# Tile 7 of a window attention joins the tiles that take small scores and a turned exchange

## The chip, the cores and the metric

The kernel runs on one core of a Trainium2 chip. The core has five engines with a queue of instructions each: TensorE (PE: matmuls, its weight loads apart as PEld), VectorE (DVE), ScalarE (ACT), GpSimd (POOL), and SyncE (SP), which here issues all DMAs. The metric is the device time of one execution in microseconds (us). Three runs of the kernel before gave 554.05, 554.26 and 555.79 us; the median is 554.26.

## The reference

q, k and v have 8 batches, 8 heads, 576 tokens and 64 columns a head. Attention looks back at most 127 tokens, with a bias that falls linearly with distance; then comes a feed-forward part with a convolution of three tokens and a gate.

```python
scores = scale * np.matmul(q, k.transpose(0, 1, 3, 2))
mask = (rel >= 0) & (rel < 128)
scores = np.where(mask, scores - slopes * abs(rel), -1e9)
attn = softmax(scores); x = np.matmul(attn, v)      # heads side by side: 512 columns
h = np.maximum(x @ w_in, 0.0)                       # 512 -> 1024
conv = cw[0] * h[s-1] + cw[1] * h[s] + cw[2] * h[s+1]
out = (h * sigmoid(conv)) @ w_out                   # 1024 -> 512
```

## The kernel before, in words

The 8 x 576 tokens are 36 tiles of 128 tokens, numbered 0 to 35. A tile's attention is done in two halves of four heads, u = 0 and 1. Two tiles form a chunk of 256 tokens for the feed-forward part, and a chunk is done in four steps s, each of two blocks of 128 hidden columns. In the names of tiles, sc is scores, e the exponentials, av the product with v, p the up product, z the gate, gh and gl the high and low part of the gated values, o the output sums. The feed-forward products run as three fp32r products (high by high, high by low, low by high).

There are two ways to do a tile's attention.

- The whole way (tiles 0 to 7 before): scores are 128x128 matmuls over the tile's own keys and, in a second set, the tile before (`scores`, L398). VectorE merges the two by masks (L442). The exponentials are normalised, TensorE transposes them (`attnT`, L507), they are copied out of PSUM (`attn_out`), POOL selects what belongs to which tile (`select`), and TensorE multiplies with v over 128 keys (`av`, L631).
- The turned way (tiles 8 to 35 before): scores are matmuls of 32 queries over 160 keys (`scores_window`, L413), so that each query block sees the 160 keys that its window can touch. VectorE turns the exponentials in blocks of 32 (`turn_e`, L534), they are written to DRAM (`write_e`, L544: 1 MB) and read back in another arrangement by four DMAs (`swap_e`, L558), POOL selects (`select_e`, L568 and L572), and TensorE multiplies with v in quarters of the array (`av_quarters`, L591). The two halves of the sum are added on VectorE (`x_sum`, L605).

A third piece belongs to the turned tiles: q and k come as 32-row blocks and VectorE turns them (`turn`, from tile TURN on), where earlier tiles are transposed by TensorE (`qkT`).

The order of the work is written out by hand. OPENING covers tiles 0 to 10 and the weights' preparation, PERIOD is a loop over pairs of tiles from tile 8 on, TAIL the rest. Each word is a step and its arguments: S7.0 are the scores of tile 7, half 0; MP, MB its masks and bias; X exponentials; N normalisation; TE, WE, SE, CE the four steps of the exchange; AV the product with v; XA, XS, XH, XL the steps to the feed-forward input; UH up, HH relu, Z, CA and CB convolution, TH tanh, GT gate, GH and GL the high and low part, D down, OB output; F, CL, RS, LW, V, H and W weights; I a few filler matmuls; LG four loads of q and k. Each engine executes its own instructions in the order of these words, and the table OTHER says which steps run on a second engine instead of the usual one (`pick`). All DMAs stand in SP's queue, in order.

```python
def write_e(t):
    if t < FIRST:
        return
    ...
    nc.sync.dma_start(out=scrs[t][:P].rearrange("p n b f -> p n (b f)"), in_=eb)
```

FIRST (L142) is the first turned tile, and it set TURN (L289) and the loop's start too.

Of the kernel before, what the change touches and what calls it, by code (L numbers as in the profile page):

```python
# [22 lines left out]
def tile_alibi_window_attention_conv_glu(  # L23
# [855 lines left out]
    MB0.1.1 QU1.0 QU1.1 I2 QV1.0 I2 I2 LW0 MB0.1.0 S1.0 MP1.0.1 CL4 MP1.0.0 QV1.1 S1.1 MP1.1.0 MB1.1.0 MB1.0.1 QU2.1  # L879
    X0.0.0 X0.0.1 X0.1.1 X0.1.0 NR0 QV2.1 X1.1.0 N0.0 I1 I1 N0.1 X1.0.1 LW4 QU2.0 QV2.0 S2.1 MB1.0.0 CL0 S2.0  # L880
    MP1.1.1 X1.0.0 MB1.1.1 T0.1 RS4 X1.1.1 F1 CL1 LW1 MP2.1.1 MP2.0.0 MP2.0.1 NR1 T0.0 RL0.0 RL0.1 N1.1 N1.0 F2
    SEL0.0 V4 QU3.1 MB2.1.1 I1 I1 LV2 MB2.0.0 QV3.1 MP2.1.0 MB2.1.0 MB2.0.1 RS0 QU3.0 QV3.0 T1.1 P4 S3.1 SEL0.1
    MP3.1.0 MP3.1.1 RL1.1 MB3.1.0 SEL1.1 V0 S3.0 T1.0 RL1.0 LD4 QU4.0 X2.0.1 MB3.1.1 W4 I2 X2.1.1 CL2 MP3.0.1 X2.1.0
    QU4.1 LV0 X2.0.0 NR2 N2.1 N2.0 F3 AV0 XH0 QV4.1 QV4.0 MB3.0.1 H0 T2.0 RL2.0 LW3 X3.1.1 S4.0 MP3.0.0 MB3.0.0 T2.1
    LD5 S4.1 SEL1.0 CL3 SEL2.0 MP4.0.1 MB4.0.1 RL2.1 RS1 V1 RS3 RS2 LW2 MP4.0.0 SEL2.1 QU5.1 LV1 AV1 QV5.1 AV2 F6
    CL6 S5.1 XH1 QU5.0 MP4.1.0 MB4.1.0 X3.0.0 V3 X3.0.1 F8 MP4.1.1 MB4.1.1 MB4.0.0 CL8 X3.1.0 V2 F5 CL5 XH2 XL2 H1
    QV5.0 RS8 W1 LG4 UH1.0 NR3 N3.0 N3.1 MP5.1.1 UH1.1 X4.0.1 MP5.1.0 T3.1 HH1.0 X4.1.0 MB5.1.1 UH0.0 F7 CL7 LW5 W0
    MB5.1.0 F15 HH0.0 LW8 X4.1.1 X4.0.0 NR4 RL3.1 RS6 LD6 QU6.1 LW6 V6 LW7 RS7 V7 T3.0 QV6.1 V8 N4.0 LG4 LV4 RS5 V5
    HH1.1 RL3.0 SEL3.0 UH0.1 S5.0 MP5.0.0 HH0.1 LV3 F10 CL10 Z0.1 QU6.0 MP5.0.1 H7 F9 Z0.0 T4.0 RL4.0 H3 CA0.1 CB0.1
    LG4 UH3.0 HH3.0 N4.1 UH2.0 SEL4.0 CA0.0 T4.1 CB0.0 MB5.0.1 LD7 CL9 SEL3.1 X5.1.1 QV6.0 S6.0 MB5.0.0 HH2.0 TH0  # L890
    RL4.1 RS10 SEL4.1 X5.1.0 GT0 MP6.0.0 S6.1 MB6.0.0 Z1.0 MP6.0.1 AV3 H2 W3 X5.0.0 LW10 LG4 MP6.1.1 Z1.1 MB6.0.1
    LW9 AV4 H8 QU7.1 CA1.0 CB1.0 F12 LG4 X5.0.1 MP6.1.0 MB6.1.0 CA1.1 W2 CB1.1 NR5 N5.1 LV5 UH3.1 XH4 XL4 RS9 V9
    MB6.1.1 GL0 XH3 F11 TH1 LG4 LG4 X6.0.0 UH2.1 CL15 HH2.1 Z2.1 XL3 XF4 GT1 F13 LG4 QV7.1 Z2.0 F14 X6.1.1 H6 QU7.0
    QV7.0 CL11 RS11 LW11 V10 T5.1 CA2.0 CB2.0 RL5.1 W7 LG4 W8 HH3.1 UH4.1 UH4.0 CA2.1 CB2.1 TH2 CL12 F16 S7.1 RS12
    MP7.1.1 S7.0 X6.0.1 HH4 D0 GT2 GL1 Z3.1 N5.0 T5.0 MP7.0.1 W6 MB7.0.1 UH5.0 SEL5.1 UH5.1 H5 W5 UH7.0 CA3.1 KC7
    N6.0 LW15 UH7.1 Z3.0 CL16 CA3.0 CB3.0 CL13 LW12 CB3.1 MP7.0.0 MB7.0.0 TH3 GT3 LW16 Z4.1 GL3 CL14 LG4 MP7.1.0 V12
    LG4 HH5 MB7.1.0 X7.0.0 X6.1.0 V11 N6.1 LV8 MB7.1.1 LG4 H10 LW13 LV6 W10 RS16 BW1 UH6.1 CA4.1 CB4.1 Z4.0 X7.1.0
    CA4.0 CB4.0 T6.0 TQ8 LG4 X7.0.1 RL5.0 LG4 UH6.0 TH4 GT4 LG4 LG4 GL2 LG4 SEL5.0 RL6.0 SEL6.0 V16 H16 T6.1 RL6.1
    SEL6.1 LW14 LG4 LG4 Z5.1 CA5.1 LG4 LG4 CB5.1 RS14 HH6 Z5.0 CA5.0 D1 CB5.0 RS15 RS13 AV5 XH5 HH7 GH4 BW0 V13 XL5
    V14 N7.0 AV6 XH6 TH5 GT5 Z6.0 S8.0 D2 LV9 H9 Z6.1 MP8.1.1 MB8.1.1 MP8.1.0 H12 V15 H15 LG4 LG4 CA6.1 MB8.1.0 T7.0  # L900
    RL7.0 D3 CB6.1 XL6 UH8.1 UH8.0 LG4 TQ9 X8.1.0 CA6.0 CB6.0 H14 UH9.1 W16 MP8.0.0 MB8.0.0 H11 W11 TH6 GT6 W9 H13
    GL4 Z7.1 CA7.1 CB7.1 MP8.0.1 Z7.0 HH8 MB8.0.1 W14 CA7.0 GH5 CB7.0 W13 X8.1.1 GL5 N8.1 TE8.1 S9.0 MP9.1.0 MP9.0.1
    X8.0.1 UH9.0 OB3 MP9.1.1 X7.1.1 D4 N7.1 MB9.0.1 MB9.1.1 X8.0.0 N8.0 UH10.0 GH6 W12 LV7 HH9 TE8.0 TH7 MB9.1.0
    X9.1.0 GL6 GT7 GH7 MP9.0.0 MB9.0.0 Z8.0 X9.1.1 KC9 CA8.0 T7.1 RL7.1 SEL7.1 Z8.1 X9.0.0 W15 TQ10 X9.0.1 WE8 CB8.0
    SEL7.0 GL7 N9.1 UH10.1 CA8.1 CB8.1 D5 S10.0 MP10.1.1 N9.0 MP10.0.1 D6 MP10.1.0 MB10.1.0 TH8 GT8 MB10.1.1 Z9.1
    X10.1.1 CA9.1 MP10.0.0 CB9.1 TE9.1 SE8 GH8 GL8 D7 X10.1.0 Z9.0 CA9.0 OB7 TE9.0 CE8.0 CE8.1 CB9.0 WE9 N10.1 TH9
    GT9
# [4 lines left out]
    Z0.1 CA0.1 D-2 XA0 XH-1 XL-1 XS0 CB0.1 TE2.1 XH0 XL0 TE2.0 TH0 GT0 GH0 S3.0 MP3.1.1 MB3.1.1 Z1.0 LG4 TQ4 LV3 XF0
    Z1.1 CA1.0 D-1 CB1.0 X3.1.1 CA1.1 CB1.1 LG4 UH2.1 TH1 WE2 MP3.0.1 UH2.0 HH2 Z2.1 MP3.1.0 GT1 GH1 LG4 UH3.1
    MP3.0.0 MB3.0.1 MB3.0.0 KC3 Z2.0 MB3.1.0 CA2.1 CB2.1 CA2.0 GL0 GL1 UH3.0 HH3 CB2.0 UH4.1 SE1 S4.0 MP4.1.1
    MP4.1.0 X3.0.0 X3.1.0 N3.1 SE2 TH2 GT2 X3.0.1 N3.0 LG4 LV2 MP4.0.1 Z3.1 Z3.0 LG4 OB27 LG4 CE1.1 MB4.1.1 CE1.0
    MB4.1.0 X4.1.0 X4.1.1 OB-2 LG4 CA3.1 CB3.1 CE2.0 D0 D1 OB1 TE3.0 LG4 CA3.0 CB3.0 TH3 UH4.0 TE3.1 MP4.0.0 WE3 LG4
# [45 lines left out]
```

## Time and profile before

| | |
|---|---|
| runs | 554.05, 554.26, 555.79 us |
| profiled execution, its own time | 554.5 us |
| its span, first to last instruction | 552.8 us |
| mean granted TensorE clock | 0.999 |
| TensorE busy | 546.0 us (99%) |
| weight loads, beside matmuls | 479.2 us (87%) |
| VectorE busy | 446.8 us (81%) |
| ScalarE busy | 384.4 us (70%) |
| GpSimd busy | 342.5 us (62%) |

Busy time of TensorE has modelled ends, so the table says only that it is seldom idle. The chain that ended last tells more: it is followed back from the last instruction, at each step to what released it, and its pieces are given with start and length. Matmuls of fp32 stand in the trace as two records each (16 matmuls are x32), those of fp32r as one.

### The profile page before, as it was taken

The page shows a single profiled execution, that of the slowest core. Times are in us where ns is not written, and L with a number is a line of the kernel's source. Part 1 is how long each engine was busy: PE and PEld are TensorE (multiplying, and loading weights), DVE is VectorE, ACT ScalarE, POOL GpSimd, SP SyncE. Part 2 cuts the span into 40 slices and gives each one's busy share as a digit, 9 for nine tenths or more (in the row PEclk, how much of TensorE's full clock was granted, in tenths as well). Part 3 has the DMA queues.
Part 4 walks back from the last instruction along what each step waited for, and adds up shares of the span by engine and source line. Part 5 has one row for each costly group of instructions (what it writes and reads, how often), then busy time and mean ns, then how long its engine had stood idle before and what let it go on. Part 6 is the DMA issues. An engine that isn't in the chain of part 4 may idle for free.

```text
span 552.8 us, 17956 instructions
## 1 busy us (share of the span) xinstructions
PE 546.0 (99%) x6689; PEld 479.2 (87%) x6689; DVE 446.8 (81%) x1505; ACT 384.4 (70%) x1149; POOL 342.5 (62%) x450
## 2 busy tenths in 40 slices
...
GB/s 209 229 242 204 202 104 81 164 156 169 157 205 142 231 156 205 184 205 169 183 201 175 196 178 207 163 219 184 190 176 205 179 162 148 159 155 1 39 0 78
DMA packets 206779, 91.39 MB, mean 165 GB/s; under 512 B 178380, under 2 KB 192996, under 8 KB 206692
## 3 DMA queue, kind: packets, MB, share of 16 engines
...
q14 instruction: 34, 0.28, 0.2%
...
## 4 chain that ended last, share of the span: by engine, by line
PE 91%; DMA 2%; DVE 2%; SPq 2%; issue 1%; ACT 0%; DVEq 0%
PE o L804 34%; PE p L697 33%; PE av L591 7%; PE sc L413 6%; PE p L692 3%; PE o L794 3%; PE av L631 3%; PE sc L398 2%; SPq L341 1%; DMA wst<-in_moe_w_in_dram 1%; PE pa L507 1%; PE pt L351 1%; DVE zp L732 1%; DMA rp_late<-in_q_dram 1%; SPq L315 0%
## 5 line engine op out<-in xcount | busy, mean ns | idle before, releaser
L697 PE MATMUL p<-ring,wi 128*128 128x256 f32 x1088 | 195.8, 282 | 0.7 <-ACT hh L709 0.7
L732 DVE SCALAR_TENSOR_TENSOR zp<-hh,cw,zp 128x256 f32<-128x256 f32 (+7 forms) x384 | 160.4, 418 | 29.2 <-ACT zp L717 19.6
L697 PEld LDWEIGHTS p<-ring,wi 128*128 128x128 f32 x1088 | 168.4, 188 | 4.9 <-ACT hh L709 1.1
L697 PE MATMUL p<-ring,wl 128*128 128x256 f32 x544 | 152.3, 280 | 0.0
L768 POOL TENSOR_TENSOR gl<-z,gh 128x512 fp32r<-128x512 f32 x63 | 81.5, 1294 | 100.9 <-ACT gh L186 68.4
L481 ACT ACTIVATE e<-e,st 128x128 f32<-128x128 f32 x288 | 111.8, 391 | 4.2 <-DVE st L473 3.1
L804 PE MATMUL o<-wo,gh 128*128 128x512 f32 x270 | 110.0, 407 | 0.0
L501 POOL TENSOR_TENSOR e<-e,st 128x512 f32<-128x512 f32 x69 | 72.2, 1056 | 58.9 <-DVE st L493 54.1
L804 PE MATMUL o<-wo,gl 128*128 128x512 f32 x270 | 105.7, 392 | 0.0
L804 PE MATMUL o<-wl,gh 128*128 128x512 f32 x270 | 105.2, 390 | 0.0
L697 PEld LDWEIGHTS p<-ring,wl 128*128 128x128 f32 x544 | 102.7, 189 | 0.0
L739 ACT ACTIVATE zp<-zp 128x512 f32<-128x512 f32 (+1 forms) x73 | 42.2, 578 | 62.9 <-DVE zp L732 61.5
L717 ACT ACTIVATE zp<-hh,cw 128x256 f32<-128x256 f32 x144 | 68.5, 476 | 20.0 <-DVE z L747 10.0
L473 DVE CUSTOM_DVE_ANT_0 e<-sc,bias 128x128 f32<-128x128 f32 x288 | 66.8, 284 | 1.7 <-PE pa L507 0.2
L747 DVE SCALAR_TENSOR_TENSOR z<-zp,hh 128x512 f32<-128x512 f32 (+1 forms) x73 | 49.0, 671 | 21.1 <-ACT zp L739 20.2
L804 PEld LDWEIGHTS o<-wo,gh 128*128 128x128 f32 x270 | 50.6, 188 | 16.6 <-issue 6.7
L804 PEld LDWEIGHTS o<-wo,gl 128*128 128x128 f32 x270 | 50.5, 187 | 11.5
L804 PEld LDWEIGHTS o<-wl,gh 128*128 128x128 f32 x270 | 50.8, 188 | 9.3
L709 ACT ACTIVATE hh<-p 128x512 f32<-128x512 f32 (+2 forms) x69 | 39.5, 572 | 25.2 <-PE p L697 20.3
L481 ACT ACTIVATION_READ_ACCUMULATOR e<-e,st 128x1 f32 x288 | 54.5, 189 | 0.0
L186 ACT CAST gh<-z 128x512 fp32r<-128x512 f32 x58 | 35.6, 614 | 15.3 <-DVE z L747 15.3
L572 POOL TENSOR_SCALAR_AFFINE_SELECT rr<-rr 128x512 f32<-128x512 f32 x56 | 40.2, 722 | 3.4
...
## 6 DMA issues: line engine op xcount, KB each, us to landing
scr<-eb SPq DMA_DIRECT2D x28, 1024.0 KB, 5.1
rr<-scr SPq DMA_DIRECT2D x112, 128.0 KB, 3.7
...
rp_late<-in_k_dram SPq DMA_DIRECT2D x192, 36.0 KB, 2.9
rp_late<-in_q_dram SPq DMA_DIRECT2D x192, 36.0 KB, 2.2
...
```

The costliest lines, as they stand in the source:

```text
L473: nc.vector.tensor_tensor_reduce(out=e[:, j, :], in0=of[:, g, :], in1=bias[:, u * HU + j, :], scale=-0.125, scalar=FAR, op0=ALU.add, op1=A ...
L481: nc.scalar.activation(out=e[:, j, :], in_=e[:, j, :], func=AF.Exp, bias=st[:, 0, j : j + 1], scale=-1.0, accum_out=st[:, 1, j : j + 1],)
L501: eng.tensor_tensor(out=e, in0=e, in1=st[:, 2, :].unsqueeze(2).to_broadcast([P, HU, P]), op=ALU.mult)
L572: nc.gpsimd.affine_select(out=r, in_=r, pattern=[[BK, 2], [0, H], [1, BK]], compare_op=ALU.is_ge, fill=0.0, base=q0, channel_multiplier=-1,)
L697: nc.tensor.matmul(ps, a[:, part], ring[:, i, cc, cols], start=cc == 0 and n == 0, stop=cc == NCC - 1 and n == 2)
L709: nc.scalar.activation(out=to, in_=ps, func=AF.Relu, scale=0.5)
L717: nc.scalar.activation(out=zps[s][:, ff, :], in_=hhs[s][:, ff, 1 : 1 + CW], func=AF.Copy, scale=cw[:, 1, f : f + 1])
L732: nc.vector.scalar_tensor_tensor(out=z[:, ff, a:cut], in0=hh[:, ff, a + kk : cut + kk], scalar=cw[:, kk, f : f + 1], in1=z[:, ff, a:cut], ...
L739: nc.scalar.activation(out=zps[s][:, ff], in_=zps[s][:, ff], func=AF.Tanh)
L747: nc.vector.scalar_tensor_tensor(out=zgs[s][:, ff], in0=zps[s][:, ff], scalar=1.0, in1=hhs[s][:, ff, 1 : 1 + CW], op0=ALU.add, op1=ALU.mult,)
L768: eng.tensor_tensor(out=gl, in0=zgs.pop(s), in1=as32(gh), op=ALU.subtract)
L804: nc.tensor.matmul(to, a[:, ff, ms], w[:, part], start=first and n == 0, stop=end and n == 2)
```

## The change

FIRST becomes 7, while TURN (which tiles' q and k are turned by VectorE) and the loop's start, now named SOLO, stay at 8. Tile 7 is then loaded and transposed as before, but takes scores over 160 keys, each half as its own step, and goes through the exchange and the quarters. Its eight attention transposes, copies and whole-tile selects go. The orders OPENING, PERIOD and TAIL and the table OTHER are new throughout; of them the diff shows some lines.

```diff
-    FIRST = 8
+    FIRST = 7
...
-    TURN = FIRST
+    TURN = 8
+    SOLO = 8
...
     def scores(t, u):
-        if t >= TURN:
-            if u == 0:
-                for half in range(2):
-                    scores_window(t, half)
+        if t >= FIRST:
+            for half in range(2) if t >= SOLO else (u,):
+                scores_window(t, half)
             return
...
-        if t >= TURN:
+        if t >= FIRST:
             place_window(t, ps)
...
-        of = pss[a][:, :, BK:WIN] if t >= TURN else pss[a][:, :, window(t)[1], :]
+        of = pss[a][:, :, BK:WIN] if t >= FIRST else pss[a][:, :, window(t)[1], :]
...
-    LH0.0 LH0.1 LD1 F0 QU0.0 QU0.1 QV0.0 S0.0 MP0.0.0 F4 MP0.0.1 MB0.0.0 QV0.1 S0.1 LD2 MP0.1.1 LD3 MB0.0.1 MP0.1.0
+    LH0.0 LH0.1 QU0.0 QU0.1 QV0.0 S0.0 QV0.1 S0.1 LD1 QU1.0 I2 QV1.0 I2 MP0.0.1 MB0.0.1 X0.0.1 MP0.1.1 MP0.0.0
...
-        for t in range(FIRST, NT, 2):
-            emit(PERIOD, t, 2 * (t - FIRST) + 10, "P:")
-        emit(TAIL, NT, 2 * (NT - FIRST) + 10, "T:")
+        for t in range(SOLO, NT, 2):
+            emit(PERIOD, t, 2 * (t - SOLO) + 10, "P:")
+        emit(TAIL, NT, 2 * (NT - SOLO) + 10, "T:")
```

Five normalisations of the opening move from GpSimd to VectorE (N4.0, N4.1, N6.0, N8.1, N9.0 and N9.1 come into OTHER, N8.0 leaves it).

SP's queue where the first exchanges stand, before (scr is the DRAM buffer, eb the turned exponentials, rr what is read back; the first number is the tile):

```order
L544 DMA scr8_1742<-eb8_1590 256x1x1024
L558 DMA rr8_1857<-scr8_1742 32x4x256 x4
L830 DMA out_0_dram<-ob1_1885 128x2x512
L544 DMA scr9_1896<-eb9_1855 256x1x1024
L315 DMA rp6_late_1998<-in_k_dram 32x9x32 x8
```

And now:

```order
L544 DMA scr7_1698<-eb7_1537 256x1x1024
L558 DMA rr7_1700<-scr7_1698 32x4x256 x4
L544 DMA scr8_1724<-eb8_1582 256x1x1024
L558 DMA rr8_1882<-scr8_1724 32x4x256 x4
L830 DMA out_0_dram<-ob1_1906 128x2x512
L544 DMA scr9_1913<-eb9_1873 256x1x1024
L316 DMA rp6_late_2118<-in_k_dram 32x9x32 x12
```

Tile 7's write and reads stand ahead of tile 8's.

VectorE's queue behind tile 9's scores, before, up to the turn of tile 8's second half (L463 masks, L473 bias, with its sums' read; L493 reciprocal, L501 normalisation, L534 turn):

```order
L463 COPY_PREDICATED sc9_1_1_1611<-w_start_124,neg_90 128x2x128
L493 RECIPROCAL st7_1_1089<-st7_1_1089 128x4
L473 ISA e9_0_1631,st9_0_1632<-sc9_0_1_1593,bias_142 128x128
L473 ISA st9_0_1632 128x1
L473 ISA e9_0_1631,st9_0_1632<-sc9_0_1_1593,bias_142 128x128
L473 ISA st9_0_1632 128x1
L473 ISA e9_1_1628,st9_1_1629<-sc9_1_1_1611,bias_142 128x128
L473 ISA st9_1_1629 128x1
L473 ISA e9_1_1628,st9_1_1629<-sc9_1_1_1611,bias_142 128x128
L473 ISA st9_1_1629 128x1
L493 RECIPROCAL st8_0_1550<-st8_0_1550 128x4
L501 TENSOR_TENSOR e8_0_1549<-e8_0_1549,st8_0_1550 128x512
```

And now, up to the turn of tile 7's second half (L732 is a convolution side):

```order
L473 ISA e9_1_1624,st9_1_1625<-sc9_1_1_1607,bias_142 128x128
L473 ISA st9_1_1625 128x1
L732 SCALAR_TENSOR_TENSOR zp7_1566<-hh3_166,cw_153,zp7_1566 128x256
L463 COPY_PREDICATED sc9_0_0_1588<-w_start_124,neg_90 128x2x128
L493 RECIPROCAL st7_1_1177<-st7_1_1177 128x4
L473 ISA e9_1_1624,st9_1_1625<-sc9_1_0_1606,bias_142 128x128
L473 ISA st9_1_1625 128x1
L473 ISA e9_1_1624,st9_1_1625<-sc9_1_0_1606,bias_142 128x128
L473 ISA st9_1_1625 128x1
L493 RECIPROCAL st8_0_1456<-st8_0_1456 128x4
L732 SCALAR_TENSOR_TENSOR zp7_1566<-hh3_166,cw_153,zp7_1566 128x256
L534 STREAM_TRANSPOSE eb7_1537<-e7_1_1176 128x4x4x32
```

Tile 7's turn stands behind the reciprocal of tile 7's second half, which POOL's normalisation follows; two masks and two more bias rows of tile 9 come ahead of the part shown.

## Rows read from the trace of the kernel before

**Rows 1.** The page's list of busy time by engine.
```profile
PE 546.0 (99%) x6689; PEld 479.2 (87%) x6689; DVE 446.8 (81%) x1505; ACT 384.4 (70%) x1149; POOL 342.5 (62%) x450
```

**Rows 2.** TensorE's waits: us in total, times, longest.
```profile
PE idle L72 <- DVE x_first L275: 1.1, 1, 1.1
PE pt L351 <- DVE st L473: 1.1, 1, 1.1
PE p L697 <- ACT hh L709: 0.7, 2, 0.4
PE pt L351 <- DVE rl L188: 0.3, 1, 0.3
```

**Rows 3.** The chain, 60 to 130 us: start, length, engine, tile, line, count.
```profile
64.48 2.29 PE sc L398 x32
...
87.32 1.25 PE sc L413 x64
...
92.20 0.44 PE pa L507 x4
...
103.18 2.75 PE o L804 x12
105.93 1.42 PE p L697 x12
...
118.89 2.83 PE p L697 x24
121.72 1.90 PE av L631 x32
...
125.12 2.96 PE o L804 x12
```

**Rows 4.** The chain over the whole span.
```profile
50.86 1.99 PE sc L398 x32
...
160.26 7.08 PE p L697 x60
...
178.56 2.84 PE av L591 x128
```

**Rows 5.** Busy time in three stretches: engines in us (x instructions), clock, DMA.
```profile
40.00:100.00 60.00, 60.00 (x535) 48.68 (x534) 55.34 (x160) 48.23 (x134) 45.75 (x62) 1.00 0.65 143
200.00:300.00 100.00, 99.66 (x1425) 88.10 (x1424) 80.28 (x270) 72.56 (x218) 66.67 (x86) 1.00 0.71 182
300.00:400.00 100.00, 99.39 (x1349) 88.16 (x1349) 80.10 (x283) 70.69 (x221) 61.37 (x79) 1.00 0.73 192
```

**Rows 6.** SP's queue in order of time: start, length of issuing.
```profile
106.96 0.58 SPq L544 DMA_DIRECT2D scr<-eb  x1
111.25 1.76 SPq L558 DMA_DIRECT2D rr<-scr  x4
```

**Rows 7.** VectorE in order of time, 102 to 108 us.
```profile
102.59 0.71 DVE L534 STREAM_TRANSPOSE eb<-e 128x512 f32<-128x512 f32 x1 [1.22 <-POOL e L501]
103.23 1.22 DVE L463 COPY_PREDICATED_SCALAR sc<-w_start,neg 128x256 f32 x3
```

**Rows 8.** VectorE's groups by form: count, busy us, mean ns, idle before.
```profile
L732 DVE SCALAR_TENSOR_TENSOR zp<-hh,cw,zp 128x256 f32<-128x256 f32 x176 | 85.2, 484 | 15.4 <-ACT zp L717 11.3
L473 DVE CUSTOM_DVE_ANT_0 e<-sc,bias 128x128 f32<-128x128 f32 x288 | 66.8, 284 | 1.7 <-PE pa L507 0.2
...
L501 DVE TENSOR_TENSOR e<-e,st 128x512 f32<-128x512 f32 x3 | 2.1, 702 | 0.1
```

**Rows 9.** POOL in order of time, 119 to 123 us.
```profile
119.69 0.73 POOL L568 TENSOR_SCALAR_AFFINE_SELECT ll<-rr 128x512 f32<-128x512 f32 x1
...
122.64 1.04 POOL L501 TENSOR_TENSOR e<-e,st 128x512 f32<-128x512 f32 x1
```

**Rows 10.** The page's DMA issues: KB each, median us to landing.
```profile
scr<-eb SPq DMA_DIRECT2D x28, 1024.0 KB, 5.1
rr<-scr SPq DMA_DIRECT2D x112, 128.0 KB, 3.7
```

More of the change, by code (lines that the diff above doesn't have):

```diff
@@ L870, in tile_alibi_window_attention_conv_glu @@
         """
-        GH6 GH7 GH8 GL5 H14 H15 H16 H2 H5 H9 HH0.0 HH3.1 HH4 HH5 KC7 LW0 LW1 LW10 LW14 LW4 LW8 N2.0 N3.1 N8.0
-        QV2.0 QV3.0 RL1.0 RL3.1 RL5.1 RL6.1 T:GH-1 T:GH0 T:GH1 T:GH2 T:GH3 T:GH4 T:GH5.0 T:GH5.1 T:GL-1 T:GL0
-        T:GL4 T:GL5.0 T:HH0 T:HH2 T:HH4 T:HH5.1 T:XL-1 W11 W13 W14 W9 XH0 XH2 XH6
+        GH5 GH7 GH8 GL5 GL7 H11 H14 H15 H5 H7 H8 H9 HH0.0 HH1.0 HH3.0 KC7 LW10 LW14 LW15 LW4 N2.0 N3.1 N4.0 N4.1
+        N6.0 N8.1 N9.0 N9.1 P:GH-1 QV3.1 QV4.0 RL1.0 RL2.0 RL3.1 RL4.1 RL6.1 T:GH2 T:GH3 T:GH5.0 T:GH5.1 T:GL-1
+        T:GL2 T:HH0 T:HH4 T:HH5.1 T:OB5 T:XA-1 W1 W15 W6 W9 XH2
         """.split()
@@ L877, in tile_alibi_window_attention_conv_glu @@
     OPENING = """
-    LH0.0 LH0.1 LD1 F0 QU0.0 QU0.1 QV0.0 S0.0 MP0.0.0 F4 MP0.0.1 MB0.0.0 QV0.1 S0.1 LD2 MP0.1.1 LD3 MB0.0.1 MP0.1.0
[L879 to L907, printed above, removed]
+    LH0.0 LH0.1 QU0.0 QU0.1 QV0.0 S0.0 QV0.1 S0.1 LD1 QU1.0 I2 QV1.0 I2 MP0.0.1 MB0.0.1 X0.0.1 MP0.1.1 MP0.0.0
@@ new lines, in tile_alibi_window_attention_conv_glu @@
+    MB0.0.0 QU1.1 QV1.1 S1.1 S1.0 MB0.1.1 LD2 QU2.0 X0.0.0 MP0.1.0 MB0.1.0 QU2.1 X0.1.1 F4 CL4 X0.1.0 F0 MP1.1.0
+    MB1.1.0 LW4 I2 NR0 QV2.1 I1 MP1.0.0 N0.1 MB1.0.0 I1 X1.1.0 S2.1 LV2 MP1.0.1 N0.0 MB1.0.1 MP1.1.1 MP2.1.0 MP2.1.1
+    T0.0 QV2.0 LD3 F2 CL0 RS4 MB1.1.1 QU3.1 X1.0.1 F1 X1.0.0 QU3.0 MB2.1.1 V4 P4 X1.1.1 NR1 S2.0 MP2.0.0 LD4 I1 T0.1
+    I1 I2 N1.1 RL0.0 QV3.1 MB2.0.0 S3.1 LV0 QV3.0 T1.1 F3 S3.0 MB2.1.0 RS0 LW0 V0 MP3.1.1 LV1 X2.0.0 QU4.0 CL2 RS2
+    LD5 MP3.1.0 MB3.1.0 MP2.0.1 SEL0.0 MB3.1.1 N1.0 W4 MB2.0.1 RL0.1 SEL0.1 RL1.1 X2.1.0 T1.0 SEL1.1 AV0 X2.1.1
@@ new lines, in tile_alibi_window_attention_conv_glu @@
+    QV4.0 RL1.0 QU4.1 X2.0.1 NR2 N2.0 T2.0 LW1 XH0 F8 QV4.1 S4.0 S4.1 CL1 RS1 MP3.0.0 MP3.0.1 X3.1.0 MB3.0.1 X3.0.1
+    N2.1 T2.1 RL2.0 CL3 RS3 SEL1.0 F6 RL2.1 LG4 MP4.0.1 MB4.0.1 SEL2.0 LW2 QU5.1 MB3.0.0 X3.0.0 V1 QV5.1 MP4.1.1
+    MP4.1.0 H1 LW3 MP4.0.0 MB4.1.0 MB4.0.0 AV1 XH1 MB4.1.1 X3.1.1 SEL2.1 AV2 V3 LW6 XH2 V2 F5 X4.0.0 CL8 RS8 F7 CL6
+    CL5 XL2 NR3 N3.0 N3.1 S5.1 QU5.0 UH1.0 LG4 HH1.0 RS6 QV5.0 UH1.1 MP5.1.1 CL7 X4.0.1 MP5.1.0 H0 T3.1 H3 MB5.1.1
+    RL3.1 LW8 X4.1.0 RS7 F15 UH0.0 LD6 QU6.1 QU6.0 W1 HH0.0 LV4 X4.1.1 NR4 MB5.1.0 N4.1 RS5 LW7 LG4 LW5 HH1.1 UH0.1
@@ new lines, in tile_alibi_window_attention_conv_glu @@
+    V7 QV6.1 F10 N4.0 V5 HH0.1 Z0.1 V8 T3.0 RL3.0 W0 SEL3.0 S5.0 QV6.0 H7 T4.0 V6 UH3.0 RL4.0 SEL4.0 LV3 CL10 H8
+    Z0.0 MP5.0.0 MP5.0.1 MB5.0.1 CA0.0 CB0.0 F9 LG4 X5.1.1 MB5.0.0 X5.1.0 CA0.1 H2 UH2.0 HH2.0 S6.0 HH3.0 S6.1
+    MP6.0.0 X5.0.1 CB0.1 MB6.0.0 SEL3.1 LW9 MP6.0.1 F11 TH0 X5.0.0 T4.1 RL4.1 GT0 MB6.0.1 H6 LG4 AV3 MP6.1.0 NR5 F12
+    SEL4.1 AV4 CL9 N5.1 LW10 UH3.1 Z1.1 Z1.0 CA1.0 RS10 UH2.1 XH3 LW15 LD7 QU7.0 XL3 CA1.1 CB1.1 LV5 LG4 W6 CB1.0
+    N5.0 XH4 XL4 X6.0.0 LW11 XF4 TH1 MP6.1.1 GT1 HH3.1 T5.1 MB6.1.0 HH2.1 Z2.1 CA2.1 RL5.1 RS9 W2 W3 CB2.1 V9 UH4.1
@@ new lines, in tile_alibi_window_attention_conv_glu @@
+    BW0 QV7.0 X6.0.1 MB6.1.1 F13 QU7.1 CL11 Z2.0 CA2.0 CB2.0 UH5.0 S7.0 X6.1.1 MP7.0.1 V10 W7 LG4 GL0 TH2 GT2 GL1
+    BW1 QV7.1 LG4 LG4 RS11 H5 Z3.1 Z3.0 F16 LG4 LW12 X6.1.0 W8 MP7.0.0 MB7.0.0 D0 W5 CA3.1 CB3.1 SEL5.1 F14 UH4.0
+    HH4 S7.1 CA3.0 CB3.0 V11 TH3 MB7.0.1 MP7.1.0 GT3 LG4 LG4 KC7 UH7.0 CL16 N6.0 X7.0.0 Z4.0 CA4.0 T5.0 RL5.0 N6.1
+    LV6 Z4.1 UH5.1 UH6.0 RS16 CA4.1 HH5 MP7.1.1 MB7.1.1 TQ8 CB4.0 LG4 LW16 LG4 CL13 MB7.1.0 H10 UH7.1 LG4 LG4 T6.0
+    CB4.1 RS13 UH6.1 CL15 RS15 LG4 TH4 LG4 T6.1 LG4 LW13 CL12 RS12 GL3 GT4 RL6.0 SEL5.0 AV5 RL6.1 SEL6.1 Z5.0 CA5.0
```

33 lines of the change are left out of this document (21 added, 12 removed).

## Prediction

> **What bounds the kernel now.** I read the page's list of engines first: TensorE is busy 546.0 of 552.8 us [rows 1]. Matmul ends are modelled there, so I did not trust it alone and asked next what TensorE waited for: 3.4 us in all, with three waits (1.1, 1.1 and 0.3) before 25 us, one of 0.4 on ACT's relu near 95 us, and little after it [rows 2]. Then the chain that ended last: from about 60 us on it stays on TensorE, and its pieces follow each other without holes, so the length of a piece there is its price [rows 3]. In the steady loop the same pieces return with the same lengths: 7.08 for 60 up-matmuls, 2.84 for two tiles of quarters [rows 4]. So the program is as long as TensorE's work plus the waits left in the opening and the tail. A change pays here only as TensorE time, and what comes too late for TensorE is lost one for one.
>
> The profiled execution took 554.5 us, 1.7 more than its span; the median of the runs is 554.26, 0.24 less. I sum against 554.5 and take the 0.24 off at the end.
>
> **TensorE's own work.** Loading tile 7 and turning its q and k stay as they are (TURN is still 8). Four things change on TensorE.
> 1. Scores. The 16 matmuls over 128 keys took 2.29 for tile 7 itself [rows 3] and 1.99 for another tile [rows 4] (two records a matmul); 32 small ones over 160 keys take 1.25 [rows 3]. Saved 0.74 to 1.04, I take 0.9.
> 2. The eight transposes of tile 7's attention go: two pieces of 0.44, one of which is shown [rows 3]. Saved 0.88.
> 3. Attention times v: 1.90 for tile 7 whole [rows 3], 1.42 in quarters (half of 2.84) [rows 4]. Saved 0.48.
> 4. Returns from small array tiles to full ones. Twelve down-matmuls right after small ones take 2.96, others 2.75 [rows 3]: 0.2 a return. Along TensorE's order from tile 1's v product to the loop, the new order has three more: the two halves of tile 7's scores stand apart, tiles 5 and 6 no longer run their v products together, and tile 6's scores are parted from tile 3's v product. Added 0.6.
> Net: 0.6 - 0.9 - 0.88 - 0.48 = -1.66; between -1.8 and -1.5 by the two prices of the scores.
>
> The Trainium skill (TensorEngine Tiling (Array Packing), Tiling Modes) says that changing the tiling mode, and not only the tile, drains the array. The trace shows the way back at 0.2, but 60 up-matmuls that run into scores take their plain 7.08, five times 1.42 [rows 3, 4], so the way in costs nothing that shows. If it cost as much as the way back, the three extra pairs would come to 1.2 and the net to -1.06; the rows decide, and I keep -1.66.
>
> **The loop and the tail.** In the loop TensorE's blocks stand in the same order as before; only the other engines' orders differ. Each block already has its plain length, so a new order can win no more there than the 0.95 that TensorE was idle in two windows of 100 us [rows 5]; a worse one can lose. The tightest new place is the copy of the last half of g (GH1), which ACT now does behind two exponentials of the next tile, though the 12 down-matmuls of the step before (2.75) cover it. I take 0, from -0.95 to +0.95. The tail keeps its full-size blocks in another order: 0. Its last copy of outputs goes to VectorE for the first row half, beside matmuls of the second.
>
> **What becomes late: tile 8's exchange.** Tile 8 had the queue SP for itself: write issued at 106.96, reads at 111.25, 4.29 later, their issue 1.76 long [rows 6]. Now tile 7's write and reads stand ahead, and SP takes them in order: tile 8's write waits behind tile 7's reads, and these until tile 7's write has landed. Count from the end of tile 9's scores.
> VectorE does three masks (1.13, from 103.23 less the overlap) [rows 7], two bias additions (0.28 each) and one convolution side (0.48) [rows 8]: 2.2, and a reciprocal of 0.1. POOL scales (1.04) [rows 9], VectorE turns (0.64 to the next start) [rows 7]: write 7 goes at 4.0. Reads 7 start at 8.3 and are out by 10.1. Write 8 goes at 10.1, reads 8 from 14.4, the fourth of them 1.3 later and 3.7 to landing [rows 10]: 19.4. POOL's four selects take 2.95 (119.69 to 122.64) [rows 9]: tile 8 is ready at 22.4.
> TensorE has, in its new order, between the same point and tile 8's v product: 24 up with a return (3.0), 12 down (2.75), 12 up (1.42), scores (1.25), 12 down (2.96), 12 up (1.42), 24 down (5.5), 24 up (2.83), tile 7's quarters (1.42): 22.6 [rows 3, 4]. It just fits, or not: with the page's median of 5.1 for a write [rows 10] the two writes come 1.6 later, and write 8 now shares the DMA engines with reads 7. TensorE would stand there with everything behind it. I take 0.5, from 0 to 2.0.
>
> **The start.** Up to about 30 us the order is new: tile 2's q and k are fetched ahead of the first weights, the fillers on TensorE (as many) stand elsewhere, and VectorE gives two of the first weight shifts to ACT. Two of the waits lie there, 1.1 and 0.3; the other 1.1, at the very start, nothing touches [rows 2]. With the 0.4 near 95 us I take -0.4 for all of them, between -1.8 (all three go) and +1.5 (one more of the largest size, and a small one).
>
> Sum: 554.5 - 1.66 + 0.5 - 0.4 = 552.94; less 0.24 is 552.7.
>
> **Rivals.**
> A. The new opening removes those waits and the exchange is in time: 554.26 - 1.66 - 1.8 = 550.8. For it: all three waits lie where the order is new. Against: they are on VectorE and ACT, and VectorE is nearly full right behind them.
> B. The exchange of tile 8 is 2.0 late and eats the gain: 554.26 - 1.66 + 2.0 - 0.4 = 554.2. For it: the 5.1 of the page. Against: the write in this very stretch took 4.29.
> C. Slower: VectorE becomes the bound of the opening. From 40 to 100 us it is busy 55.34 of 60 [rows 5]. It gets five more normalisations (0.70 each [rows 8]), two turns, a sum and a copy out of PSUM, nine in all, and loses seven of like size and 0.8 in masks: some 0.6 more, in a stretch that should get 1.7 shorter. Its hole of 1.22 before tile 8's turn [rows 7] was a wait for POOL's normalisation, which VectorE now does itself. If TensorE has to follow it, the gain is gone, 0.6 comes on top and tile 8 waits 2.0: 554.26 + 0.6 + 2.0 = 556.9. It decides when VectorE has no hole left ahead of tile 9's scores. Against: from 40 to 100 us TensorE shows no idle time of its own [rows 5].
> That the change doesn't act is out: the transposes of tile 7's attention are gone from TensorE's order.
>
> **Chances.** Forecast 0.50 (its own range 551.6 to 554.1), A 0.20, B 0.15, C 0.15. A measurement of this kernel tells 0.3% (1.66 us) from nothing: faster is below 552.6, slower above 555.9. Faster: nearly half of the forecast (0.23) and A: 0.43. Slower: C with a little of B, 0.16. Same: 0.41. The range, 550.5 to 556.6, takes in A and most of C.
>
> **What would show it.** Right: the chain has 64 records of small scores for tile 7 and no pieces of four attention transposes between 85 and 110 us; the first quarters are those of tiles 7 and 8, with at most about 1 us of wait between them; the loop's pieces are unchanged. Wrong: TensorE waits more than 2 us for POOL's selects, or for VectorE between 40 and 100 us, or the loop's period is longer than the sum of its pieces.

## The result: slower by 1.2%

Four runs of the changed kernel gave 559.68, 560.96, 561.42 and 561.59 us, median 561.19, against 554.15 for the kernel before on the same chip: ratio 1.0115, 95% interval 1.0092 to 1.0139. Forecast were 552.7, with 550.5 to 556.6: the time lies outside, on the side that was given 0.16. The profiled execution of after is the fastest of its runs (559.68, span 558.0); it shows 5.2 us of the loss, and the other runs took 1.3 to 1.9 longer.

The page's busy times of after, answering to [rows 1]:

```profile
PE 545.8 (98%) x6745; PEld 476.0 (85%) x6745; DVE 449.5 (81%) x1508; ACT 382.8 (69%) x1140; POOL 346.9 (62%) x458
```

TensorE is as busy as before in a span 5.2 longer. So the sum shows nothing of the saved work, and what was added is waiting. TensorE's waits of after (total, times, longest), answering to [rows 2]:

```profile
PE sc L413 <- DVE qkT_all L366: 1.8, 1, 1.8
PE idle L72 <- DVE x_first L275: 1.1, 1, 1.1
PE pt L352 <- DMA rp<-in_k_dram: 1.0, 2, 0.6
PE sc L413 <- DVE xx L605: 0.9, 1, 0.9
PE sc L398 <- ACT qkT_all L186: 0.7, 1, 0.7
PE pa L507 <- DVE st L473: 0.7, 1, 0.7
PE av L591 <- POOL rr L572: 0.5, 1, 0.5
...
PE p L697 <- POOL wl L244: 0.4, 1, 0.4
PE p L697 <- POOL ring L665: 0.3, 1, 0.3
```

Two of these were in no part of the forecast. The larger is tile 10's scores, which wait for VectorE's turn of tile 10's q and k. The chain of after, 60 to 130 us, answering to [rows 3], shows what made that turn late:

```profile
104.57 1.05 POOL e L501
105.64 0.71 DVE eb L534
...
107.66 1.44 DVE gl L768
109.20 0.69 DVE z L747
109.89 1.16 DVE qkT_all L366
111.05 0.14 issue
111.19 1.32 PE sc L413 x64
...
125.22 1.50 PE av L591 x64
126.75 1.57 PE av L591 x64
```

VectorE turns tile 7's second half (eb) when POOL has normalised it, then does a low part (gl) and a gate (z), and only then the turn that TensorE needs. Before, this chain stayed on TensorE all the way. The other is `wl`: the chain of after, 58 to 75 us, runs over POOL:

```profile
59.76 2.92 POOL wl L244 x2
...
67.50 1.50 POOL bias L268 x2
...
70.28 0.61 POOL wi L188
70.89 2.98 POOL wl L244 x2
73.87 0.04 issue
73.91 1.10 PE p L697 x7
```

The turned scores need the bias in its wide form (L268), eight instructions and some 5 us of POOL. For tile 8 they could come late; for tile 7 they come at 62 to 70 us, between the low parts of weights that TensorE waits for.

What I feared most was in time here. SP's queue of after, answering to [rows 6], has tile 7's write and reads, then tile 8's:

```profile
106.38 0.58 SPq L544 DMA_DIRECT2D scr<-eb  x1
111.29 1.76 SPq L558 DMA_DIRECT2D rr<-scr  x4
113.15 0.55 SPq L544 DMA_DIRECT2D scr<-eb  x1
119.44 1.73 SPq L558 DMA_DIRECT2D rr<-scr  x4
```

Tile 8's quarters follow tile 7's with no hole (125.22 + 1.50, then 126.75), but because TensorE came late itself: tile 7's v product began at 121.72 before and at 125.22 now (this mark by the chain; by the list of TensorE's instructions, which the other runs are compared by, 121.66 and 125.15). In the second profile of the same kernel (e8) TensorE waits 0.5 for tile 8's selects.

A ledger of the profiled executions, by TensorE's idle time: up to 32 us 3.9 against 2.6 before; from 32 to 100 us 1.1 against 0.0, of it 0.5 for a load at 43 us and 0.4 for POOL at 73 us; the turn at 109 us 1.8; together 4.1 more. The mark is 3.5 later, so TensorE's busy time up to it fell by 0.6, where the sum counted 1.18 (1.66 less 0.48). From the mark to the end 1.7 is added, nearly all in the loop: from the last quarters to the end it is 40.0 after 39.9. Busy time from the start to the quarters of the loop's first pair (PE, PEld, DVE, ACT, POOL; granted clock; DMA), in before, in after, and in e10, a later run with tile 7's change in the old orders:

```profile
0.00:150.69 150.69, 148.06 (x1516) 125.56 (x1516) 133.84 (x486) 116.47 (x367) 103.82 (x141) 1.00 0.71 172
0.00:153.99 153.99, 147.17 (x1571) 122.55 (x1571) 135.68 (x489) 117.90 (x371) 100.57 (x139) 1.00 0.72 177
0.00:149.89 149.89, 146.88 (x1572) 124.09 (x1572) 133.86 (x487) 116.71 (x374) 101.66 (x135) 1.00 0.74 182
```

### The profile page after: what moved, and what is told of

It is laid out like the page before. It is cut to its first block, busy times and chain, and to the rows that moved or that the text cites. A ratio compares the mean times of both kernels' runs of the same rounds, so it can differ in the third digit from the quotient of the medians.

```text
span 558.0 us, 18098 instructions
## 1 busy us (share of the span) xinstructions
PE 545.8 (98%) x6745; PEld 476.0 (85%) x6745; DVE 449.5 (81%) x1508; ACT 382.8 (69%) x1140; POOL 346.9 (62%) x458
## 4 chain that ended last, share of the span: by engine, by line
PE 85%; POOL 5%; DVE 4%; SPq 2%; DMA 2%; issue 1%; ACT 0%; POOLq 0%; DVEq 0%
PE o L804 32%; PE p L697 31%; PE av L591 7%; PE sc L413 6%; PE sc L398 2%; PE o L794 2%; PE av L631 1%; POOL wl L244 1%; DMA rp<-in_k_dram 1%; SPq L316 1%; PE p L692 1%; PE pa L507 1%; POOL bias L268 1%; PE pt L352 1%; POOL e L501 1%
## 5 line engine op out<-in xcount | busy, mean ns | idle before, releaser
L732 DVE SCALAR_TENSOR_TENSOR zp<-hh,cw,zp 128x256 f32<-128x256 f32 (+7 forms) x384 | 160.8, 419 | 37.4 <-ACT zp L717 28.9
L501 POOL TENSOR_TENSOR e<-e,st 128x512 f32<-128x512 f32 x64 | 67.7, 1066 | 32.4 <-DVE st L493 29.7
L473 DVE CUSTOM_DVE_ANT_0 e<-sc,bias 128x128 f32<-128x128 f32 x288 | 68.9, 286 | 1.9 <-POOL e L501 0.2
L709 ACT ACTIVATE hh<-p 128x512 f32<-128x512 f32 (+2 forms) x71 | 40.9, 580 | 20.9 <-PE p L697 17.9
L568 POOL TENSOR_SCALAR_AFFINE_SELECT ll<-rr 128x512 f32<-128x512 f32 x52 | 37.5, 721 | 13.1 <-DMA rr<-scr 13.0
L572 POOL TENSOR_SCALAR_AFFINE_SELECT rr<-rr 128x512 f32<-128x512 f32 x58 | 41.6, 721 | 3.6
```

The costliest lines, as they stand in the source:

```text
L473: nc.vector.tensor_tensor_reduce(out=e[:, j, :], in0=of[:, g, :], in1=bias[:, u * HU + j, :], scale=-0.125, scalar=FAR, op0=ALU.add, op1=A ...
L501: eng.tensor_tensor(out=e, in0=e, in1=st[:, 2, :].unsqueeze(2).to_broadcast([P, HU, P]), op=ALU.mult)
L572: nc.gpsimd.affine_select(out=r, in_=r, pattern=[[BK, 2], [0, H], [1, BK]], compare_op=ALU.is_ge, fill=0.0, base=q0, channel_multiplier=-1,)
L709: nc.scalar.activation(out=to, in_=ps, func=AF.Relu, scale=0.5)
L732: nc.vector.scalar_tensor_tensor(out=z[:, ff, a:cut], in0=hh[:, ff, a + kk : cut + kk], scalar=cw[:, kk, f : f + 1], in1=z[:, ff, a:cut], ...
```

## The experiments

Medians and ratios are against the kernel before on the same chip in the same session; its median lay between 553.64 and 555.02. Where an edit moves words, the diff shows those words alone.

**Opening or loop?** e1 is the changed kernel with the loop and tail of before; e2 is before with the loop and tail of after.

```diff
 e1 (on after)                    e2 (on before)
-    PERIOD, TAIL: after's       -    PERIOD, TAIL: before's
+    PERIOD, TAIL: before's      +    PERIOD, TAIL: after's
```

> The changed kernel with the steady loop and tail (PERIOD, TAIL, their words of OTHER) in the old order: the new opening alone. Theory (the new opening's order costs most: TensorE reached the loop's first scores 3.5 us late, 131.58 after 128.08, and the loop and tail added 1.7): 557.5 to 559.5, so 1.7 under the changed kernel. Rival (the loop's new order costs most, the late start is taken up later): 555 or less.

> The kernel before with only the loop and tail in the new order, tile 7 as it was. Theory: the loop's new order alone loses about 1.7 us (TensorE's new waits at 187.9, 193.0, 354.5 and 416.6 us of the changed kernel, 3.0 in all, less 1.3 of such waits before): 555.4 to 556.2. Rival (those waits only follow from the late opening, the order is harmless): 554.2 within 0.5.

e1: 557.43, ratio 1.0060 (1.0039 to 1.0081), just under the theory's 557.5. The new opening costs about half of the loss; with the old loop none of TensorE's waits in the loop is above 0.3, so the loop's new order costs the other half when it follows this opening. e2: 560.26, 1.0103 (1.0074 to 1.0133), more than theory or rival said. Three of its six runs took 561.6 to 561.7, the others 558.1 to 559.0; the profile is of one of the shorter (558.38), and what the longer ones add no trace shows. This trace shows mainly one place, at the loop's first pair (a second, 1.1 us, is at 353 us). TensorE's waits of e2:

```profile
PE p L697 <- DVE ring L665: 3.6, 1, 3.6
```

and the stretches behind it (PE, PEld, DVE, ACT, POOL busy; granted clock; DMA):

```profile
130.00:132.00 2.00, 1.58 (x7) 0.94 (x6) 1.89 (x5) 0.03 (x1) 0.00 (x0) 1.00 0.73 253
133.00:134.00 1.00, 0.00 (x0) 0.00 (x0) 0.89 (x4) 0.47 (x3) 0.00 (x0) 1.00 1.04 284
136.00:137.00 1.00, 1.00 (x6) 1.00 (x6) 0.78 (x8) 0.00 (x0) 0.00 (x0) 0.50 0.90 236
138.00:139.00 1.00, 1.00 (x10) 1.00 (x10) 0.00 (x0) 0.00 (x0) 0.00 (x0) 1.00 0.97 210
```

TensorE stands for 3.6 us and comes back at a granted clock of 0.50 (1.2 of 2.4 GHz) until 138 us: 6 matmuls in a microsecond where 10 follow. The seam between an opening and a loop that were not ordered together is dear twice over, by the wait and by the clock behind it. The Trainium skill (TensorE: Matmul & The Clock Gate, Part 1: The HAM clock gate) says that a monitor of TensorE's activity halves its clock when it has idled; the trace agrees, with 0.50 behind the 3.6 us. Idleness of 1.76 us at 109 us in after, and of 2.1 us at 31 us in e5, left the clock at 1.00.

**The loop without the seam.** e15 is before with the first pair of the loop in the old order and the other pairs in the new one.

```diff
-            emit(PERIOD, t, 2 * (t - FIRST) + 10, "P:")
+            emit(PERIOD if t == FIRST else LATER, ...)    # LATER: after's PERIOD
```

> The kernel before with the loop's first pair of tiles in the old order and the other 13 in the new one, tail old. Theory (e2's 3.6 us at 131 us and the low clock behind it belong to the seam between old opening and new loop; the new loop itself loses the 1.7 us seen in the changed kernel): 1.2 to 2.2 over before. Rival (only the seam costs): within 0.5 of before.

554.12, 0.9994 (0.9977 to 1.0012), the rival: the loop's new order by itself costs nothing, and its profile has no wait of TensorE above 0.3 behind 50 us (its tail is the old one). So the loop's 1.7 (and the more of the medians) belongs to the combination: new loop behind new opening. Whether its first pair in the new order does it, or the queues that the new opening leaves, no run separates.

**Is it always so?** e8 is the changed kernel again.

```diff
 (no edit)
```

> The changed kernel unaltered, profiled again, because its first profile (559.68) was the fastest of four runs (to 561.59). Theory (the waits of the new loop come from transfers whose time varies, on top of a fixed late opening): av of tiles 7 and 8 starts within 0.5 of 125.2 us again, and the loop's waits lie elsewhere or are longer, 1.7 to 4 in all. Rival (the opening itself varies by 2 us from run to run): av starts 1 us or more apart from 125.2.

559.77, 1.0116 (1.0094 to 1.0138). Tile 7's v product starts at 124.84 (125.15 in the first profile), with the same 1.76 at 109 us, and the loop's waits stand at the same places, 188, 192, 354 and 417 us, of other sizes. The opening's loss is the same within 0.4; the loop's places are the same too, where the theory expected others.

**The start.** e5 puts the start of before ahead of the new opening, e14 the start of after ahead of the opening of before.

```diff
 e5 (on e1): OPENING                        e14 (on before): OPENING
-    LH0.0 LH0.1 QU0.0 ... S4.0 S4.1      -    LH0.0 LH0.1 LD1 F0 ... LD5 S4.1
+    LH0.0 LH0.1 LD1 F0 ... LD5 S4.1      +    LH0.0 LH0.1 QU0.0 ... S4.0 S4.1
```

> As e1 (new opening, old loop and tail), but the opening's first 137 words, to the scores of tile 4 at 36 us, in the old order. Theory (TensorE's waits up to 32 us, 2.7 in e1's profile and 1.8 before, and the load it waits for at 43 us add up along the path, for TensorE never gets them back): about 1 to 1.6 under e1's 557.4, so 555.8 to 556.5. Rival (the middle of the opening is bound by VectorE and POOL, which give an earlier start no use): 557 to 557.8, as e1.

> The kernel before with only the opening's first 129 words, to the scores of tile 4, in the new order; tile 7 as it was. Theory (the new start loses about 1.6 us: waits of 3.5 up to 32 us in the changed kernel's profile, 1.8 before): 1.0 to 1.7 over before. Rival (an early loss is given back where VectorE and POOL bound the opening): within 0.5 of before.

e5: 558.50, 1.0094 (1.0076 to 1.0113), slower than e1; the splice made a wait of its own (2.1 us at 31 us ahead of a v product), so it tells nothing of the start. e14: 555.71, 1.0018 (1.0003 to 1.0034); tile 8's quarters begin 1.4 later than before and the last output block 1.3, as the theory said. TensorE's three largest waits in e14 behind the first 2 us:

```profile
PE pt L351 <- DVE st L473: 0.8, 1, 0.8
PE sc L398 <- ACT qkT_all L186: 0.7, 1, 0.7
PE pt L351 <- DMA rp<-in_k_dram: 0.3, 1, 0.3
```

But the largest of them stands right behind the seam, where after has none:

```profile
36.85 0.66 PE L351 MATMUL pt<-ident_r,rp 128*128 128x128 f32 x4 [0.80 <-DVE st L473]
```

Tile 4's scores, the last of the new start, begin at 34.90 in e14 and at 34.49 in before, so the start itself has cost 0.4 there and the seam the rest. In after they begin at 35.61, 1.1 late, with no wait behind them; in five more profiles with the new start and opening (e1, e4, e6, e8, e11) 0.9 to 1.5 late.

**The turn of tile 10.** e4 moves it on the changed kernel; e6 moves the last bias of tile 9 too, on e1.

```diff
-    GL5 HH9 GL6 GT7 WE7 SE7 TQ10 D4 MB9.0.0
+    TQ10 GL5 HH9 GL6 GT7 WE7 SE7 D4 MB9.0.0        (e4)
+    MB9.0.0 TQ10 GL5 HH9 GL6 GT7 WE7 SE7 D4        (e6)
```

> The changed kernel with one step moved: VectorE turns tile 10's q and k ahead of the low part GL5 and the gate Z7, not behind them. Theory: TensorE's single largest wait, 1.8 us ahead of tile 10's scores, is set by this place in VectorE's queue and goes, with nothing late in its place: 1.5 to 1.8 under the changed kernel, 558.0 to 559.7. Rival (the wait is taken up by a following one, GL5 being 1.2 later for the down-matmuls, or by the loop): within 0.5 of the changed kernel.

> As e1, with tile 10's turn and the last bias of tile 9 (MB9.0.0) both ahead of GL5 on VectorE. Theory (e4 took away one wait ahead of tile 10's scores and met the next, 1.4 us for that bias, which frees the PSUM tile): both go, 1.5 to 1.8 under e1: 555.6 to 556.0. Rival (VectorE's queue as a whole is late there, so what is pushed back, GL5, Z7 and tile 7's turned write, stalls TensorE instead): within 0.5 of e1's 557.4.

e4: 559.46, 1.0086 (1.0062 to 1.0111), within the theory's numbers, but not as it said: tile 10's scores still wait 1.1 us, now for the bias (L473) that frees their PSUM tile. e6: 557.15, 1.0063 (1.0047 to 1.0079): no better than e1. Tile 7's v product starts 1.6 earlier than in e1 (123.04 after 124.61), and inside it TensorE waits for ACT's relu (hh):

```profile
PE av L591 <- ACT hh L709: 0.7, 1, 0.7
```

By 128 us 1.2 of the 1.6 is given back, so my theory fell and the rival's kind of end came true, at another place than it named. The wait for the turn itself is gone: its place in VectorE's queue was the cause.

**Tile 7's change alone.** e3 has the changed functions in the old orders; e7 adds three cures.

```diff
 e3 (on before's OPENING, with FIRST = 7)
-    S7.1 ... N7.0 ... T7.0 RL7.0 ... N7.1 ... T7.1 RL7.1 SEL7.1 ... SEL7.0
+    S7.1 BW1 BW0 ... N7.0 N7.1 ... TE7.0 TE7.1 WE7 ... SE7 OB3 ... CE7.0 ... CE7.1
 e7 (on e3)
-            pick(nc.gpsimd, nc.vector).tensor_scalar(out=bias[:, h, :], in0=back, ...)
+            nc.scalar.activation(out=bias[:, h, :], in_=back, func=AF.Copy, scale=-8.0 * slope)
+    X6.0.1 BW0 ... TH3 BW1 ... N8.1 TE7.0 TE7.1 TE8.1 WE7 ... WE8 SE7 ... GL7 CE7.0 CE7.1 ... CE8.0 CE8.1 GH8
```

> Tile 7's change alone: the old orders everywhere, with tile 7's two halves normalised one behind the other, its turns and write where its first four transposes stood, its reads ahead of the first output store, its selects where the old selects stood; the bias is widened ahead of tile 7's bias, on VectorE. Theory (the change itself saves TensorE some 1.7 us, the new orders cost): 552.0 to 553.5. Rival (the change itself costs, by the exchange, the widened bias or a full VectorE): 555 or more.

> As e3 (tile 7's change in the old orders), with three cures: ScalarE widens the bias, half 0 behind the exponentials X6.0.1 and half 1 ahead of tile 7's second bias; tile 7's two turns stand in VectorE's hole of 1.2 us ahead of tile 8's turn; tile 7's reads go behind tile 8's write, and POOL's selects of tiles 7 and 8 ahead of GH8. Theory (e3's waits at 69 to 73 us, 2.5, were the 4.5 us of widening in VectorE's queue, and the turns ahead of tile 9's keys the rest, so the change costs TensorE nothing where these have room): 552.3 to 554. Rival (the opening is so full that any extra work ends at TensorE: as e3): 556 or more.

e3, in which VectorE widens the bias: 557.33, 1.0061 (1.0033 to 1.0088); the rival won. TensorE's waits from 60 to 80 us and VectorE's row of the bias in e3:

```profile
PE pa L507 <- DVE hh L711: 1.5, 1, 1.5
PE p L697 <- DVE st L473: 0.7, 1, 0.7
```

```profile
66.24 4.49 DVE L268 TENSOR_SCALAR bias<-back 128x128 f32<-128x128 f32 x8
```

The eight took 4.49 us on VectorE, single ones from 0.21 to 1.30, while POOL worked beside them. The Trainium skill (SBUF — State Buffer, section Who interferes with whom) says that VectorE in its two-port mode and GpSimd take a pair of ports by an exclusive lock, the later one waiting for a whole instruction. The trace agrees: five of the eight end 0.08 behind an instruction of POOL that ran beside them (0.61 to 1.26 long), and the three of 0.21 each begin just as one of POOL's has ended. That they run in that mode is inferred from this. In e7 ScalarE does four in 0.89:

```profile
68.12 0.89 ACT L268 ACTIVATE bias<-back 128x128 f32<-128x128 f32 x4
```

e7: 556.69, 1.0055 (1.0035 to 1.0075), the rival again. (Lines are two lower from here on.) Tile 7's v product now starts at 121.63, about where it did before, and stops after two matmuls:

```profile
PE av L589 <- ACT hh L707: 1.9, 1, 1.9
```

My reading: quarters fill two PSUM tiles, the whole product one. The second is held by an up product until its relu, and ACT's queue has the relu behind a tanh that waits for VectorE. Behind this stall the clock shows 0.50 again, at 126 to 128 us.

**The PSUM tile.** e9 is e7, e11 is e6, each with the relu of step 10 ahead of that tanh; e12 gives before two cures alone, ScalarE's widening and this one. The words of e9:

```diff
-    N10.1 TH9 GT9            (and HH0 in the loop's first pair)
+    N10.1 HH10 TH9 GT9
```

> As e7, with one step moved: ScalarE's relu of step 10 (HH10) ahead of the tanh of step 9. Theory (e7's 1.9 us wait inside tile 7's quarters, named ACT's relu, is for PSUM: quarters write two tiles where the whole product wrote one, the second is held by an up product until its relu, and that stands behind a tanh that waits for VectorE): the wait goes, 1.5 to 2.1 under e7's 556.7, so 554.6 to 555.2. Rival (the wait only hides that tile 8's exchange is late: POOL's selects for tile 8 end at 124.0, 2.4 after the quarters begin): within 0.7 of e7.

> As e6 (new opening with tile 10's turn and bias early, old loop), with the relu of step 10 ahead of the tanh of step 9. Theory (in e6 the cure at 109 us was given back at the same PSUM wait, 0.9 in the quarters at 123): 0.7 to 1.0 under e6's 557.15. Rival (given back once more behind it, in the exchange or the loop's first step): within 0.4 of e6.

> The kernel before (tile 7 the old way) with two of the cures alone: ScalarE widens the bias, and the relu of step 10 stands ahead of the tanh of step 9. Theory (these only make room for tile 7, before had no wait for them): same as before within 0.5. Rival (the cures would speed up the kernel before as well, so what e10 gains is not the change's): 1 us or more under before.

e9: 556.71, 1.0028 (1.0013 to 1.0043). By its ratio it is 0.27% better than e7, by its median no better (556.69); the intervals overlap, and the two ran on chips on which before took 555.02 and 553.64, so a gain is not shown, and the theory's 1.5 to 2.1 was missed. e11: 557.03, 1.0036 (1.0018 to 1.0054), the same beside e6 (557.15): the rival. e12: 555.06, 0.9997 (0.9981 to 1.0013): the cures give nothing where tile 7 goes the old way. In e9 and e11 the relu's wait is gone from inside tile 7's quarters, which bears out the reading, and another stands ahead of tile 8's quarters, e9 first:

```profile
PE av L589 <- POOL gh L188: 1.5, 1, 1.5
```

```profile
PE av L591 <- POOL rr L572: 0.8, 1, 0.8
```

This is the late exchange of my rival B. In e9 it is some 0.9 of the 1.5: tile 8's last select ends at 123.51, and the quarters begin at 124.13, behind POOL's next instruction (gh, 0.61), which the profile names. Why they wait for that one is not shown.

**The exchange of tile 8.** e10 has four more places mended; e13 lets tile 7's reads go ahead of tile 8's write.

```diff
 e10 (on e9)
-    X7.0.1 X7.1.1 ... SEL6.1 ... GT7 GH7 ... KC9 CA8.0 ... TQ10 ... GL7 CE7.0 CE7.1 N9.1 ... N9.0
+    X7.0.1 ... SEL6.1 X7.1.1 ... GT7 KC9 GH7 ... TQ10 CA8.0 ... GL7 N9.1 ... N9.0 CE7.0 CE7.1
 e13 (on e10)
-    WE8 SE7 CB8.0 GL7 N9.1 ... N9.0 CE7.0 CE7.1
+    SE7 WE8 CB8.0 GL7 CE7.0 CE7.1 N9.1 ... N9.0
```

> As e9, with tile 7's last exponentials behind the selects of tile 6, POOL's normalisations of tile 9 ahead of the selects of tile 7, and tile 9's copy of keys and tile 10's turn earlier. Theory (the change itself saves 1.66 us of TensorE, the rest is order, and e7's remaining new waits were 0.7 at 86 us, 0.4 at 111 and POOL's selects): 552.0 to 553.3 against 553.6 to 554.1 before. Rival (with the turned tile VectorE and POOL are the bound, each cure moves the wait): 555 or more.

> As e10, with tile 7's reads ahead of tile 8's write in SP's queue, and POOL's selects of tile 7 ahead of its normalisations of tile 9. Theory (e10's 0.9 us ahead of tile 8's quarters comes from eight selects in a row on POOL, 5.9 us, which begin when tile 7's reads have landed, 5.6 after their issue because tile 8's 1 MB write goes ahead of them): the reads land some 4 us earlier, the wait goes, and TensorE reaches tile 8's quarters 0.7 to 1.0 earlier: 0.997 to 0.999 of before. Rival (tile 8's write then goes later and its own reads make the quarters late): tile 8's quarters no earlier than in e10, 1.000 or more.

e10: 555.16, 1.0000 (0.9977 to 1.0023), the rival's number. TensorE starts tile 7's v product at 120.01, 1.65 earlier than before, and the quarters of the loop's first pair at 149.89, 0.80 earlier; between them lies a wait of 0.7 ahead of tile 8's quarters. The lead does not last: the quarters of the loop's third pair begin 0.44 later than before (207.20 after 206.76), in the loop's old order; one wait of 0.3 lies between, and the rest is not followed. (Its profiled run is the slowest of twelve: a load that landed late at 307 us, in a loop whose order is that of before, cost 3.5 us and the clock behind it.) SP and POOL in e10:

```profile
106.79 0.55 SPq L542 DMA_DIRECT2D scr<-eb  x1
107.44 7.77 SPq L556 DMA_DIRECT2D rr<-scr  x8
```

```profile
115.96 0.72 POOL L566 TENSOR_SCALAR_AFFINE_SELECT ll<-rr 128x512 f32<-128x512 f32 x1 [0.27 <-DMA rr<-scr]
...
121.14 0.72 POOL L570 TENSOR_SCALAR_AFFINE_SELECT rr<-rr 128x512 f32<-128x512 f32 x1
```

Tile 7's reads are issued from 107.44 on, right behind tile 8's write, and land just behind it, from 113.05 on; eight selects then run to 121.86, and tile 8's quarters begin at 122.56, again behind POOL's gh. e13: 554.61, 0.9996 (0.9978 to 1.0013). The reads issued at 108.39 land from 111.96 on, but tile 8's write now waits behind them:

```profile
108.39 1.79 SPq L556 DMA_DIRECT2D rr<-scr  x4
110.28 0.55 SPq L542 DMA_DIRECT2D scr<-eb  x1
116.15 1.73 SPq L556 DMA_DIRECT2D rr<-scr  x4
```

```profile
120.56 0.72 POOL L566 TENSOR_SCALAR_AFFINE_SELECT ll<-rr 128x512 f32<-128x512 f32 x1 [1.70 <-DMA rr<-scr]
...
122.81 0.72 POOL L570 TENSOR_SCALAR_AFFINE_SELECT rr<-rr 128x512 f32<-128x512 f32 x1
```

Tile 8's selects end at 123.5, and the wait ahead of its quarters is 0.74 again, here for the last select, and they begin later than in e10 (123.61): the rival. Either order costs the same by the ratios; my account of it is that two exchanges of this size so close behind each other share one queue and one engine for the selects. No version here beats the kernel before by more than its interval.

## Why the prediction was wrong

- **TensorE's own work, -1.66: only in part.** The eight attention transposes are gone, and tile 7's quarters take 1.50 where the whole product took 1.90 [rows 3]. But TensorE's busy time up to the quarters of the loop's first pair fell from 148.06 to 147.17 in after and to 147.94 in e8, and runs with tile 7 the old way have 147.67 to 147.97 (e12, e14, e15) beside the 148.06. With the old orders it is 146.47 to 146.88 (e9, e10, e13). Against 147.9, the mean of those four old ones, 1.0 to 1.4 was saved there, and in the new opening 0 to 0.7. The three dearer returns to full array tiles were not measured by themselves, and what took the rest in the new opening stays open.
- **The start, -0.4: wrong in sign.** I let the two waits of the old start go and bounded the worst case by one more of them. The new start has more waits, each smaller, and costs 1.1 in after, which is inside that bound. The 0.4 near 95 us was misread: both waits for the relu in [rows 2] lie in the loop, at 279 and 308 us.
- **Waits in the middle: a term that was missing.** I read the 55 us of VectorE in 60 [rows 5] and set rival C on the hole ahead of tile 9's scores [rows 7]. VectorE has no such hole left (0.29 ahead of tile 7's turn), and it is VectorE's queue that TensorE follows at 109 us, for 1.8. The mechanism was C's, with a chance of 0.15; its price of 0.6 counted VectorE's added work, where what cost was the place of one turn in its queue (e6 moves it, and the wait is gone). That place could be read from the order of instructions before the run: gl and z stand ahead of the turn that the next scores need.
- **The wide bias: a step that I didn't see.** Its deadline moves from tile 8's bias to tile 7's, and its place with it, from 78 to 87 us before to 62 to 70 us in after, where POOL has no room. Waits beside it are 2.2 in e3, and 0.4 at 73 us in after, by the chain alone: no run moved it in the new opening.
- **Tile 8's exchange, +0.5: right in kind.** In after it hides behind the lateness of TensorE (0.5 shows in e8); where that is cured waits of 0.7 to 1.5 show (e9, e10, e13), inside my 0 to 2.0, though in e9 and e10 0.6 to 0.7 of them stands behind gh, not behind a select. The sum was short by the write: I counted 4.29 for tile 8's, and in after its reads start 6.29 after it (113.15 to 119.44).
- **The two PSUM tiles of the quarters: not seen.** I priced quarters by TensorE's time alone. They cost 1.9 in e7 and 0.7 in e6.
- **The loop, 0 with ±0.95: right for the order, wrong for the whole.** Alone it costs nothing (e15); behind the new opening it costs 1.7 in the profile and some 3 us by the ratios of after and e1. I took the loop's blocks on TensorE for the loop, and left out that its first pairs may inherit queues of ACT, POOL and SP from what stands ahead. In after the chain at 188 to 193 us runs over POOL. Why the waits come back at 354 and 417 us has not been followed to its end; it stays open.

The step that failed is thus the sum's silence on the queues of the other engines: it gave the middle of the opening no wait and the loop none, where the runs show 1.8 for one turn on VectorE and 1.7 in the loop, with 1.1 for a start that was to give 0.4. Of the 1.66 that was to pay, 0.6 shows at tile 7's v product. With the old orders and the late steps mended that the traces named (e10, e13) what remains is below what a measurement tells from nothing: the change removes work from TensorE and gives it to queues that were already the second bound.
